# FFT and two expert layers on one core: a tensor constant in the weight conversion, sums of expert 2 kept in PSUM

## Chip, core and metric

The kernel runs on one core of one Trainium2 chip, as a single program. The metric is the device time of one execution in microseconds (us). TensorE (PE) multiplies matrices, with its weight loads (PEld) beside them; VectorE (DVE), ScalarE (ACT) and GpSimd (POOL) work element by element; SyncE (SP) issues the DMAs. Each engine takes its instructions in order and waits on semaphores. Matmuls write to PSUM, eight banks of 128 partitions x 512 fp32; everything else lives in SBUF.

## The reference

```python
X = np.fft.fft(np.fft.fft(x, axis=1), axis=2).real      # x: (2, 3008, 256)
x = X.reshape(6016, 256)
h = x @ w_in                                            # expert 1: 256 -> 2048
x = (h / (1 + np.exp(-h))) @ w_out                      # silu, 2048 -> 256
h = x @ w_in2                                           # expert 2
y = (np.maximum(h, 0) + alpha * np.minimum(h, 0)) @ w_out2
```

The weights come as float64.

## The kernel before

The kernel holds everything transposed, features on partitions and tokens along the free dimension. A value that must keep fp32 accuracy is split into a high and a low part (`hi`, a rounded copy made by ScalarE; `lo`, the difference, made by VectorE or GpSimd), and a product is three matmuls: hi by hi, hi by lo, lo by hi.

**Stages.** The DFT of batch 0 takes the first 40 us. Expert 1 runs from there to about 448 us, as 96 steps of 16 feature tiles x 6 token chunks of `CW` = 502 columns; in it the DFT of batch 1 and all weight conversions are spread by a table of step numbers (`PLAN`), and a scheduler orders each engine's instructions. Expert 2 runs from 448 us to the end, in an order written out by hand.

**Conversion from float64** (`to_f32`). A weight block of 128x512 arrives as two 32-bit words for each value. Five steps make fp32 of it: `zero` (ScalarE: absolute value of the high word), `one` (VectorE: maximum with a constant), `two` (VectorE: shift left by 3 and mask), `three` and `four` (VectorE: or in bits of the low word, then the sign). There are 32 such conversions of a block: 16 of expert 1's weights (tiles `cvi`, `cvo`), between 17 and 166 us, and 16 of expert 2's (`v2w`, `v2o`), between 258 and 415 us. Expert 1's steps meanwhile need VectorE three times each: `t` (from the PSUM tile `pe`), `hp` and again `t` (from `po`); GpSimd makes `gl`, the low parts, most of the time.

**Expert 2.** There are 96 passes of the loop, each for one pair of feature tiles `n`. The first layer is a fast 2x2 block product: seven block products (`product(n, j, ...)`, three matmuls of 252 columns each) in place of eight, with block sums formed by the other engines. All of pass `n` shares one bank `ac` (two halves of 252 columns) and uses one more, `b`:

- `outer(n)`: products 1 and 5 into the halves of `ac`; ScalarE copies both halves to `e` in SBUF.
- `inner(n)`: product 2 into `b`, product 6 added to the first half of `ac`, product 3 to the second. `h11`: VectorE adds `b` and `e` to a part of `h0`. `h12`: ScalarE copies the first half of `ac` to `u`, then VectorE adds it to the second half, into the other part of `h0`.
- `seventh(n)`: product 7 onto the first half of `ac`, then copied to `u`; `h22`: VectorE adds `u` and `e` into a part of `h1`. `fourth(n)`, in the next pass: product 4 onto the first half of `ac`, which is the rest of `h1`.
- `absolute` and `prelu`: the activation as a*h + |b*h|, |b*h| (`q`) by ScalarE, the sum by VectorE; once for `h0` (502 columns) and twice for `h1` (252 columns out of SBUF, 250 straight out of `ac`).
- `high2`, `low2`: the split of the result (`gh`, `gl`); `mm4`: the second layer, 12 matmuls of 502 columns in each pass, into two banks that are written out (`ot`, `out_t`) every eight passes.

In each pass TensorE issues: products 1 and 5, six matmuls of the second layer, product 4 of the pair before, products 2, 6 and 3, six matmuls of the second layer, product 7.

Of the kernel before, what the change touches and what calls it, by code (L numbers as in the profile page):

```python
# [122 lines left out]
def fft_moe_kernel(  # L123
# [337 lines left out]
    def prep_o1(g):  # L461
        pieces = []

        def high(h, v):
# [8 lines left out]
        for h in range(2):
            v, st = to_f32(None, (f"o{g}", h * 512, 512), f"o{g}_{h}")
# [241 lines left out]
    W = CW - HALF  # L716

    def outer(n):

        h = H[n] = {}  # L720
        h["ac"] = mm_ps(f"ac{n}", 2 * HALF)
# [2 lines left out]
        h["e"] = work(F32, f"e{n}", 2 * HALF)
        nc.scalar.activation(h["e"], h["ac"], AF.Copy)

    def inner(n):

        h = H[n]
        h["b"] = mm_ps(f"b{n}", HALF)  # L730
        product(n, 2, h["b"], True)
# [2 lines left out]
        h["u"] = work(F32, f"u{n}", 2 * HALF)
        h["h0"] = work(F32, f"h0_{n}")

    def h11(n):
        h = H[n]
        nc.vector.tensor_tensor(h["h0"][:, :W], h["b"][:, :W], h["e"][:, :W], op=ALU.add)

    def h12(n):
        h = H[n]
        nc.scalar.activation(h["u"][:, :HALF], h["ac"][:, :HALF], AF.Copy)  # L743
        nc.vector.tensor_tensor(h["h0"][:, R], h["ac"][:, HALF:], h["u"][:, :HALF], op=ALU.add)

# [13 lines left out]
    PART = {0: (0, slice(0, CW)), 1: (1, R), 2: (1, slice(0, W))}  # L759

    def source(n, part):
        i, to = PART[part]
        return H[n]["ac"][:, :W] if part == 2 else H[n][f"h{i}"][:, to]

    def absolute(n, part):

        i, to = PART[part]
        h = H[n]
        if ("q", i) not in h:
            h["q", i] = work(F32, f"q{i}_{n}")  # L770
        nc.scalar.activation(h["q", i][:, to], source(n, part), AF.Abs, scale=coef(n, i, 1))  # L771

    def prelu(n, part):
        i, to = PART[part]
# [49 lines left out]
    if True:  # L824
        with tc.manual_schedule():
            zero = conv(F32, "zero")
            nc.vector.memset(zero[:, :256], 0.0)
# [132 lines left out]
        with tc.manual_schedule():  # L960
# [102 lines left out]
```

## Time and profile before

| | us |
|---|---|
| median of 3 runs | 961.2 (961.08 to 964.77) |
| the profiled execution, its own time | 962.4 |
| its span, first to last instruction | 960.5 |
| PE busy | 948.8 (99%) |
| DVE busy | 791.4 (82%) |
| ACT busy | 708.0 (74%) |
| POOL busy | 418.2 (44%) |

The chain of work that ended last is PE for 87% of the span. A matmul's recorded duration contains its latency, and the next one starts before it ends, so PE's work is read better from the distance between starts: two matmuls of 502 columns start 0.23 us apart, two of 252 columns 0.115 us. The granted clock of TensorE is 0.999 of full speed over the span.

### The profile page before, as it was taken

Reading aid. Unit: us, or ns where it says so; the run is one execution under the profiler, and the core shown is the slowest. Engines: PE = TensorE matmul, PEld = TensorE weight load, DVE = VectorE, ACT = ScalarE, POOL = GpSimd, SP = SyncE. Lnnn points to the kernel's source line nnn. Section 1 sums busy time; section 2 is a strip of 40 time slices with the busy share of each in tenths; the row PEclk is TensorE's granted clock in tenths of the full one; section 3 lists DMA queues with packets and bytes.
Section 4 is the critical chain, followed back from the end, with each engine's and each line's share of the span. In section 5 each row is a group of like instructions: output and inputs, shape, how many; then the busy total and the mean of one; then the engine's idle time right before and its main releaser. Section 6 shows DMA issues by size and latency. Waiting matters only on the chain.

```text
span 960.5 us, 14540 instructions
## 1 busy us (share of the span) xinstructions
PE 948.8 (99%) x5236; PEld 823.8 (86%) x5236; DVE 791.4 (82%) x1334; ACT 708.0 (74%) x1413; POOL 418.2 (44%) x363
## 2 busy tenths in 40 slices
PE   9999999999999999999999999999999999999998
PEld 6887887788888888888899999999999999999997
DVE  6889999987778888996978888787878878787876
ACT  3676756675566766686888788788878888887885
POOL 2376969953266776798622122122212212221200
PEclk9999999999999999999999999999999999999999
DMA  8811110207121311100200100020020001000000
GB/s 273 251 71 44 45 45 4 83 14 234 46 102 45 118 58 43 44 0 1 86 1 23 63 3 23 1 66 14 9 65 1 23 1 65 23 1 22 1 22 22
DMA packets 17767, 49.39 MB, mean 51 GB/s; under 512 B 1824, under 2 KB 11296, under 8 KB 15648
## 3 DMA queue, kind: packets, MB, share of 16 engines
q1 hardware_dynamic: 17696, 48.47, 15.0%
q8 instruction: 41, 0.67, 0.3%
q14 instruction: 30, 0.25, 0.1%
HBM read 32.98 MB, written 15.48 MB: 50 GB/s over the span
## 4 chain that ended last, share of the span: by engine, by line
PE 87%; DVE 4%; POOL 2%; ACT 2%; DMA 2%; issue 2%; SPq 1%; ACTq 0%; POOLq 0%; DVEq 0%
PE a L807 27%; PE ac L709 20%; PE a L635 8%; PE a L637 8%; PE a L639 8%; PE b L709 3%; PE po L576 2%; PE po L578 2%; PE pe L576 2%; PE pe L578 2%; PE pe L577 2%; PE po L577 2%; DMA ys<-ya 1%; POOL gl L613 1%; PE psb L330 1%
## 5 line engine op out<-in xcount | busy, mean ns | idle before, releaser
L807 PE MATMUL a<-gh,wo 128*128 128x502 f32 x768 | 268.2, 391 | 0.0
L807 PEld LDWEIGHTS a<-gh,wo 128*128 128x128 f32 x768 | 144.9, 189 | 23.0
L613 POOL TENSOR_TENSOR gl<-t,gh 128x502 fp32r<-128x502 f32 x96 | 133.2, 1388 | 58.5 <-ACT t L601 46.4
L776 DVE SCALAR_TENSOR_TENSOR h<-h,fc,q 128x502 f32<-128x502 f32 x192 | 124.9, 650 | 33.9 <-ACT q L771 30.4
L807 PE MATMUL a<-gl,wo 128*128 128x502 f32 x384 | 149.8, 391 | 0.1
L787 DVE TENSOR_TENSOR gl<-h,gh 128x502 fp32r<-128x502 f32 x192 | 146.2, 762 | 0.1
L600 ACT ACTIVATE gh<-hp 128x502 fp32r<-128x502 f32 x96 | 59.9, 624 | 105.8 <-DVE hp L594 105.5
L637 PE MATMUL a<-gl,wo 128*128 128x502 f32 x384 | 133.7, 391 | 0.1
L639 PE MATMUL a<-gh,wo 128*128 128x502 f32 x384 | 133.4, 391 | 0.0
L635 PE MATMUL a<-gh,wo 128*128 128x502 f32 x384 | 124.3, 391 | 0.6 <-DVE o L644 0.4
L782 ACT ACTIVATE gh<-h 128x502 fp32r<-128x502 f32 x192 | 118.4, 617 | 2.9 <-DVE h L776 2.8
L771 ACT ACTIVATE q<-h,fc 128x502 f32<-128x502 f32 x192 | 116.9, 609 | 2.4 <-DVE h L754 1.3
L613 POOL TENSOR_TENSOR gl<-hp,gh 128x502 fp32r<-128x502 f32 x63 | 88.9, 1411 | 57.2 <-ACT hp L601 45.9
L591 DVE SCALAR_TENSOR_TENSOR t<-n,sm,pe 128x502 f32<-128x502 f32 x96 | 70.2, 731 | 24.6 <-PE pe L578 23.6
L695 POOL TENSOR_TENSOR os<-o1r,os 128x252 fp32r<-128x252 f32 x36 | 33.1, 933 | 122.6 <-ACT os L694 122.6
L637 PEld LDWEIGHTS a<-gl,wo 128*128 128x128 f32 x384 | 72.4, 189 | 15.7 <-POOL gl L613 0.9
L635 PEld LDWEIGHTS a<-gh,wo 128*128 128x128 f32 x384 | 71.8, 189 | 15.5 <-ACT hp L601 0.8
L639 PEld LDWEIGHTS a<-gh,wo 128*128 128x128 f32 x384 | 72.4, 189 | 14.6
L685 POOL TENSOR_TENSOR xt<-o1r 128x252 f32<-128x252 f32 x24 | 17.7, 742 | 154.1 <-DVE h L776 150.5
L807 PEld LDWEIGHTS a<-gl,wo 128*128 128x128 f32 x384 | 72.5, 189 | 8.4 <-DVE gl L787 0.6
L743 ACT ACTIVATE u<-ac 128x252 f32<-128x252 f32 x96 | 36.6, 382 | 54.4 <-PE ac L709 54.4
L594 DVE TENSOR_TENSOR hp<-t,po 128x502 f32<-128x502 f32 x96 | 64.5, 672 | 12.6 <-PE po L578 8.5
(173 smaller groups left out, 2299.0 us busy)
## 6 DMA issues: line engine op xcount, KB each, us to landing
od<-o SPq DMA_DIRECT2D x6, 1004.0 KB, 4.8
o1r<-od SPq DMA_DIRECT2D x6, 1004.0 KB, 5.7
out_t<-ot SPq DMA_DIRECT2D x24, 251.0 KB, 2.6
x<-in_xs SPq DMA_DIRECT2D x8, 512.0 KB, 5.4
raw_w<-in_wi SPq DMA_DIRECT2D x4, 1024.0 KB, 7.8
raw_w<-in_wo SPq DMA_DIRECT2D x4, 1024.0 KB, 5.7
raw_i<-in_wi SPq DMA_DIRECT2D x3, 1024.0 KB, 4.8
raw_o<-in_wo SPq DMA_DIRECT2D x3, 1024.0 KB, 6.6
```

The lines of the kernel that those rows point to most:

```text
L591: nc.vector.scalar_tensor_tensor(t, E128[c], odd_sb[:, f : f + 1], pe, op0=ALU.mult, op1=ALU.add)
L594: nc.vector.tensor_tensor(hp, t, po, op=ALU.add)
L613: LAST["gl", i] = (nc.gpsimd if s or lo_pool(i + 1) else nc.vector).tensor_tensor(lo, h, hi.bitcast(F32), op=ALU.subtract)
L635: nc.tensor.matmul(ACC1[lb, s], hi, G[i, s][0], start=st, stop=False)
L637: nc.tensor.matmul(ACC1[lb, s], hi, G[i, s][1], start=False, stop=False)
L639: nc.tensor.matmul(ACC1[lb, s], lo, G[i, s][0], start=False, stop=sp)
L709: nc.tensor.matmul(to, w, x, start=start and q == 0, stop=q == 2, skip_group_check=True)
L771: nc.scalar.activation(h["q", i][:, to], source(n, part), AF.Abs, scale=coef(n, i, 1))
L776: nc.vector.scalar_tensor_tensor(h[f"h{i}"][:, to], source(n, part), coef(n, i, 0), h["q", i][:, to], op0=ALU.mult, op1=ALU.add)
L782: nc.scalar.activation(hi, H[n][f"h{i}"], AF.Copy)
L787: nc.vector.tensor_tensor(lo, H[n][f"h{i}"], G[n, i][0].bitcast(F32), op=ALU.subtract)
L807: nc.tensor.matmul(ACC2[lb], w[lb][j], x, start=st and first, stop=sp and last)
```

## The change

In the conversion, for all blocks but the first three, step `one` becomes a VectorE operation on two tensors (the second a constant `km` of one column, read again for each element), and step `two` takes its mask from the same constant tile. The two constants are written by two small memsets at the start.

In expert 2, ScalarE copies the first half of `ac` (product 1) to the bank `b` itself, and product 2 is accumulated there by TensorE, so `h11` is no longer needed; product 2 now comes last of the three inner ones. `h12` writes its sum into the second half of `b`, `h22` writes into the second half of `ac`. Both activations then read one bank of 504 columns; the two halves overlap by two columns, which the host removes. The second layer and the output have 504 columns in place of 502.

```diff
-    def to_f32(dst, raw, n):
+    def to_f32(dst, raw, n, alone=False):
...
         def one():
             t = box[0].bitcast(F32)
-            nc.vector.tensor_scalar(t, t, F64_AT_F32_ZERO, None, op0=ALU.max)
+            if alone:
+                nc.vector.tensor_scalar(t, t, F64_AT_F32_ZERO, None, op0=ALU.max)
+            else:
+                nc.vector.tensor_tensor(t, t, km[:, :1].to_broadcast([128, w]), op=ALU.max)
 
         def two():
             t = box[0]
-            nc.vector.tensor_scalar(t, t, 3, 0x3FFFFFF8, op0=ALU.logical_shift_left, op1=ALU.bitwise_and)
...
+                mask = km.bitcast(U32)[:, 1:2].to_broadcast([128, w])
+                nc.vector.scalar_tensor_tensor(
+                    t, t, 3, mask, op0=ALU.logical_shift_left, op1=ALU.bitwise_and
+                )
...
-        h["e"] = work(F32, f"e{n}", 2 * HALF)
-        nc.scalar.activation(h["e"], h["ac"], AF.Copy)
+        h["e"] = work(F32, f"e{n}", HALF)
+        nc.scalar.activation(h["b"][:, :HALF], h["ac"][:, :HALF], AF.Copy)
+        nc.scalar.activation(h["e"], h["ac"][:, HALF:], AF.Copy)
...
-        h["b"] = mm_ps(f"b{n}", HALF)
-        product(n, 2, h["b"], True)
         product(n, 6, h["ac"][:, :HALF], False)
         product(n, 3, h["ac"][:, HALF:], False)
...
+        product(n, 2, h["b"][:, :HALF], False)
-    def h11(n):
-        h = H[n]
-        nc.vector.tensor_tensor(h["h0"][:, :W], h["b"][:, :W], h["e"][:, :W], op=ALU.add)
...
-        nc.vector.tensor_tensor(h["h0"][:, R], h["ac"][:, HALF:], h["u"][:, :HALF], op=ALU.add)
+        nc.vector.tensor_tensor(h["b"][:, HALF:], h["ac"][:, HALF:], h["u"][:, :HALF], op=ALU.add)
...
-        nc.vector.tensor_tensor(h["h1"][:, R], h["u"][:, HALF:], h["e"][:, HALF:], op=ALU.add)
+        nc.vector.tensor_tensor(h["ac"][:, HALF:], h["u"][:, HALF:], h["e"], op=ALU.add)
...
+        nc.scalar.activation(h["q", i], h["b" if i == 0 else "ac"], AF.Abs, scale=coef(n, i, 1))
...
-                    absolute(n - 1, 1)
                     high2(n - 1, 0)
...
-                    prelu(n - 1, 1)
                     fourth(n - 1)
-                    absolute(n - 1, 2)
+                    absolute(n - 1, 1)
                 if new:
                     inner(n)
-                    h11(n)
                 if old:
-                    prelu(n - 1, 2)
+                    prelu(n - 1, 1)
```

TensorE in the middle of a pass of expert 2 (pair 50; `ws0_4` are the weights of product 4, and so on; what a row waits for stands in brackets). Before:

```order
L709 MATMUL ac49_7674<-os6_0_7357,ws0_4h_3122 128x252 [waits Activation_49]
L709 MATMUL ac49_7674<-os6_1_7358,ws0_4h_3122 128x252
L709 MATMUL ac49_7674<-os6_0_7357,ws0_4l_3123 128x252
L709 MATMUL b50_7774<-os6_0_7357,ws0_2h_3655 128x252 [waits PE_49]
L709 MATMUL b50_7774<-os6_1_7358,ws0_2h_3655 128x252
L709 MATMUL b50_7774<-os6_0_7357,ws0_2l_3656 128x252
L709 MATMUL ac50_7743<-os6_0_7357,ws0_6h_4190 128x252 [waits Activation_49]
L709 MATMUL ac50_7743<-os6_1_7358,ws0_6h_4190 128x252
L709 MATMUL ac50_7743<-os6_0_7357,ws0_6l_4191 128x252
```

The same place after the change:

```order
L720 MATMUL ac49_7580<-os6_0_7273,ws0_4h_3125 128x252 [waits DVE_49]
L720 MATMUL ac49_7580<-os6_1_7274,ws0_4h_3125 128x252
L720 MATMUL ac49_7580<-os6_0_7273,ws0_4l_3126 128x252
L720 MATMUL ac50_7647<-os6_0_7273,ws0_6h_4193 128x252 [waits Activation_49]
L720 MATMUL ac50_7647<-os6_1_7274,ws0_6h_4193 128x252
L720 MATMUL ac50_7647<-os6_0_7273,ws0_6l_4194 128x252
L720 MATMUL ac50_7647<-os6_0_7273,ws0_3h_4275 128x252
L720 MATMUL ac50_7647<-os6_1_7274,ws0_3h_4275 128x252
L720 MATMUL ac50_7647<-os6_0_7273,ws0_3l_4276 128x252
L720 MATMUL b50_7648<-os6_0_7273,ws0_2h_3658 128x252 [waits PE_49]
```

Product 2 moved behind products 6 and 3, and product 4 waits for VectorE (`h22`, which now writes the same bank) where it waited for ScalarE.

VectorE in the same passes, from the `h12` of one pair to that of the next. Before:

```order
L744 TENSOR_TENSOR h0_49_7714<-ac49_7674,u49_7713 128x252 [waits Activation_49]
L787 TENSOR_TENSOR gl2_48_0_7723<-h0_48_7653,gh2_48_0_7690 128x502
L776 SCALAR_TENSOR_TENSOR h0_49_7714<-h0_49_7714,fc_82,q0_49_7721 128x502 [waits Activation_49]
L754 TENSOR_TENSOR h1_49_7753<-u49_7713,e49_7681 128x252 [waits Activation_49]
L787 TENSOR_TENSOR gl2_48_1_7755<-h1_48_7684,gh2_48_1_7719 128x502
L776 SCALAR_TENSOR_TENSOR h1_49_7753<-h1_49_7753,fc_82,q1_49_7757 128x252 [waits Activation_49]
L739 TENSOR_TENSOR h0_50_7785<-b50_7774,e50_7750 128x250 [waits PE_49]
L776 SCALAR_TENSOR_TENSOR h1_49_7753<-ac49_7674,fc_82,q1_49_7757 128x250 [waits Activation_49]
L744 TENSOR_TENSOR h0_50_7785<-ac50_7743,u50_7784 128x252 [waits Activation_49]
```

After:

```order
L748 TENSOR_TENSOR b49_7581<-ac49_7580,u49_7620 128x252 [waits PE_49,Activation_49]
L782 TENSOR_TENSOR gl2_48_0_7627<-h0_48_7591,gh2_48_0_7596 128x504
L771 SCALAR_TENSOR_TENSOR h0_49_7658<-b49_7581,fc_82,q0_49_7625 128x504 [waits Activation_49]
L757 TENSOR_TENSOR ac49_7580<-u49_7620,e49_7588 128x252 [waits Activation_49]
L782 TENSOR_TENSOR gl2_48_1_7661<-h1_48_7618,gh2_48_1_7623 128x504
L771 SCALAR_TENSOR_TENSOR h1_49_7687<-ac49_7580,fc_82,q1_49_7676 128x504 [waits Activation_49]
L748 TENSOR_TENSOR b50_7648<-ac50_7647,u50_7689 128x252 [waits PE_49,Activation_49]
```

Nine instructions became seven: the add of `b` and `e` is gone, and one activation sum of 504 columns, right in front of `h12`, stands for two of about half the size.

VectorE in expert 1, where the second block of the second group of first-layer weights (`cvi_1`) begins. Before:

```order
L187 TENSOR_SCALAR cvi_0_538<-cvi_0_538 128x512 [waits Activation_49]
L595 TENSOR_TENSOR t_523<-t_523,po_504 128x502 [waits DVE_49]
L187 TENSOR_SCALAR cvi_1_542<-cvi_1_542 128x512 [waits Activation_49]
L191 TENSOR_SCALAR cvi_0_538<-cvi_0_538 128x512 [waits DVE_49]
L350 TENSOR_TENSOR z_2_439<-psb_0_12_544,z_2_439 128x376 [waits Activation_49]
```

After:

```order
L191 TENSOR_TENSOR cvi_0_541<-cvi_0_541,km 128x512 [waits Activation_49]
L606 TENSOR_TENSOR t_526<-t_526,po_507 128x502 [waits DVE_49]
L191 TENSOR_TENSOR cvi_1_545<-cvi_1_545,km 128x512 [waits Activation_49]
L199 SCALAR_TENSOR_TENSOR cvi_0_541<-cvi_0_541,km 128x512 [waits DVE_49]
L361 TENSOR_TENSOR z_2_442<-psb_0_12_547,z_2_442 128x376 [waits Activation_49]
```

The order is the same here and the operations are of another kind; elsewhere in expert 1 the scheduler moves single instructions of VectorE and TensorE by a few places.

## Rows read from the trace of the kernel before

**Rows 1.** The profile's page, part 1: busy us, share of span, instructions.

```profile
PE 948.8 (99%) x5236; PEld 823.8 (86%) x5236; DVE 791.4 (82%) x1334; ACT 708.0 (74%) x1413; POOL 418.2 (44%) x363
```

**Rows 2.** Waits over the whole span: us in total, times, longest.

```profile
PEld ac L709 <- DVE h L744: 2.1, 3, 0.9
...
PE po L576 <- DVE t L595: 1.8, 1, 1.8
```

**Rows 3.** Busy us of each engine by stretch, then clock and DMA.

```profile
50.00:170.00 120.00, 117.24 (x552) 97.70 (x551) 111.17 (x150) 80.83 (x149) 96.00 (x77) 1.00 0.12 41
...
110.00:130.00 20.00, 20.00 (x102) 17.03 (x101) 19.10 (x28) 14.65 (x28) 16.97 (x14) 1.00 0.11 45
...
150.00:170.00 20.00, 19.08 (x93) 15.92 (x94) 19.08 (x23) 12.89 (x25) 19.53 (x15) 1.00 0.09 27
...
448.00:480.00 32.00, 31.01 (x186) 26.84 (x185) 25.27 (x48) 24.19 (x55) 18.76 (x19) 1.00 0.18 65
480.00:955.00 475.00, 475.00 (x3019) 430.64 (x3018) 381.23 (x734) 385.82 (x807) 97.49 (x95) 1.00 0.06 22
```

**Rows 4.** Timeline of one pass of expert 2: start, duration, engine, line, operation.

```profile
749.91 0.40 PE L709 MATMUL ac<-os,ws_4h 128*128 128x252 f32 x2
...
750.47 0.47 ACT L771 ACTIVATE q<-ac,fc 128x250 f32<-128x250 f32 x1 [0.22 <-PE ac L709]
...
751.15 0.47 DVE L776 SCALAR_TENSOR_TENSOR h<-ac,fc,q 128x250 f32<-128x250 f32 x1
...
751.98 0.42 DVE L744 TENSOR_TENSOR h<-ac,u 128x252 f32<-128x252 f32 x1 [0.37 <-ACT u L743]
...
752.44 0.72 ACT L771 ACTIVATE q<-h,fc 128x502 f32<-128x502 f32 x1
...
752.67 0.39 PE L709 MATMUL ac<-os,ws_7h 128*128 128x252 f32 x2
...
753.06 1.05 ACT L164 ACTIVATE ot<-a 128x502 f32<-128x502 f32 x2
...
754.00 0.38 ACT L749 ACTIVATE u<-ac 128x252 f32<-128x252 f32 x1
...
754.41 0.47 DVE L754 TENSOR_TENSOR h<-u,e 128x252 f32<-128x252 f32 x1 [0.40 <-ACT u L749]
...
755.09 0.40 PE L709 MATMUL ac<-os,ws_4h 128*128 128x252 f32 x2
```

**Rows 5.** Timeline: the one late product 7 after 480 us.

```profile
705.58 0.42 DVE L744 TENSOR_TENSOR h<-ac,u 128x252 f32<-128x252 f32 x1 [0.64 <-ACT u L743]
...
706.06 0.50 PE L709 MATMUL ac<-os,ws_7h 128*128 128x252 f32 x2
```

**Rows 6.** Groups by line and shape: busy us, mean ns of one.

```profile
L591 DVE SCALAR_TENSOR_TENSOR t<-n,sm,pe 128x502 f32<-128x502 f32 x96 | 70.2, 731 | 24.6 <-PE pe L578 23.6 <-ACT n L361 0.6
...
L725 ACT ACTIVATE e<-ac 128x504 f32<-128x504 f32 x96 | 56.7, 591 | 17.3 <-PE ac L709 16.5
...
L776 DVE SCALAR_TENSOR_TENSOR h<-ac,fc,q 128x250 f32<-128x250 f32 x96 | 44.8, 467 | 0.4 <-ACT q L771 0.4
...
L743 ACT ACTIVATE u<-ac 128x252 f32<-128x252 f32 x96 | 36.6, 382 | 54.4 <-PE ac L709 54.4
```

**Rows 7.** Timeline at the start of expert 2: `h22` and product 4.

```profile
467.95 0.95 DVE L754 TENSOR_TENSOR h<-u,e 128x252 f32<-128x252 f32 x1
...
468.21 0.40 PE L709 MATMUL ac<-os,ws_4h 128*128 128x252 f32 x2
```

**Rows 8.** Conversion steps by line: duration ns min/median/max, first and last start.

```profile
L187 DVE TENSOR_SCALAR cvo<-cvo x8: 412/856/5059, 25.1 to 152.1; 128x512 f32<-128x512 f32 x8
...
L195 DVE SCALAR_TENSOR_TENSOR cvo<-raw_o,cvo x8: 679/1106/1671, 26.0 to 160.4; 128x512 uint32<-128x512 uint32 x8
```

**Rows 9.** Timeline in expert 1: GpSimd behind a two-tensor step and behind `one`.

```profile
96.64 1.73 POOL L613 TENSOR_TENSOR gl<-t,gh 128x502 fp32r<-128x502 f32 x1
...
99.69 1.47 POOL L613 TENSOR_TENSOR gl<-hp,gh 128x502 fp32r<-128x502 f32 x1
```

More of the change, by code (lines that the diff above doesn't have):

```diff
@@ L64 @@
 PAIRS = [(k0 + i, k0 + (k1 - k0) // 2 + i) for k0, k1 in zip(K_PARTS, K_PARTS[1:]) for i in range((k1 - k0) // 2)]
+EXP_MANT = float(np.uint32(0x3FFFFFF8).view(np.float32))
 F64_AT_F32_ZERO = float(np.uint32(0x38000000).view(np.float32))
@@ L149, in work @@
     def work(dt, name, w=CW):
-        return kp.tile([128, w], dt, tag="wk", name=name, padded_shape=[128, 504])
+        return kp.tile([128, w], dt, tag="wk", name=name, padded_shape=[128, 2 * HALF])
     def conv(dt, name):
@@ L186, in one @@
             t = box[0].bitcast(F32)
-            nc.vector.tensor_scalar(t, t, F64_AT_F32_ZERO, None, op0=ALU.max)
+            if alone:
+                nc.vector.tensor_scalar(t, t, F64_AT_F32_ZERO, None, op0=ALU.max)
+            else:
+                nc.vector.tensor_tensor(t, t, km[:, :1].to_broadcast([128, w]), op=ALU.max)
         def two():
             t = box[0]
-            nc.vector.tensor_scalar(t, t, 3, 0x3FFFFFF8, op0=ALU.logical_shift_left, op1=ALU.bitwise_and)
+            if alone:
+                nc.vector.tensor_scalar(t, t, 3, 0x3FFFFFF8, op0=ALU.logical_shift_left, op1=ALU.bitwise_and)
+            else:
+                mask = km.bitcast(U32)[:, 1:2].to_broadcast([128, w])
+                nc.vector.scalar_tensor_tensor(
+                    t, t, 3, mask, op0=ALU.logical_shift_left, op1=ALU.bitwise_and
+                )
         def three():
@@ L222, in fft_moe_kernel @@
     fc = wp.tile([128, 3, NF], F32, name="fc")
+    km = wp.tile([128, 2], F32, name="km")
     cs = wp.tile([128, CD0], F32, tag="cs", name="cs")
@@ L451, in prep_w1 @@
         for h in range(2):
-            v, st = to_f32(None, (f"i{g}", 512 * h, 512), f"i{g}_{h}")
+            v, st = to_f32(None, (f"i{g}", 512 * h, 512), f"i{g}_{h}", g == 0)
             pieces.append((st, steps(h, v)))
@@ L473, in prep_o1 @@
         for h in range(2):
-            v, st = to_f32(None, (f"o{g}", h * 512, 512), f"o{g}_{h}")
+            v, st = to_f32(None, (f"o{g}", h * 512, 512), f"o{g}_{h}", g == 0 and h == 0)
             pieces.append(
@@ L714, in coef @@
         return fc[:, j, f : f + 1]
[L716 removed]
     def outer(n):
         h = H[n] = {}
[L721 removed]
+        h["ac"], h["b"] = mm_ps(f"ac{n}", 2 * HALF), mm_ps(f"b{n}", 2 * HALF)
         product(n, 1, h["ac"][:, :HALF], True)
         product(n, 5, h["ac"][:, HALF:], False)
[L724 to L725 removed]
+        h["e"] = work(F32, f"e{n}", HALF)
+        nc.scalar.activation(h["b"][:, :HALF], h["ac"][:, :HALF], AF.Copy)
+        nc.scalar.activation(h["e"], h["ac"][:, HALF:], AF.Copy)
     def inner(n):
         h = H[n]
[L730 to L731 removed]
         product(n, 6, h["ac"][:, :HALF], False)
         product(n, 3, h["ac"][:, HALF:], False)
[L734 to L739 removed]
+        product(n, 2, h["b"][:, :HALF], False)
     def h12(n):
         h = H[n]
+        h["u"] = work(F32, f"u{n}", 2 * HALF)
         nc.scalar.activation(h["u"][:, :HALF], h["ac"][:, :HALF], AF.Copy)
[L744 removed]
+        nc.vector.tensor_tensor(h["b"][:, HALF:], h["ac"][:, HALF:], h["u"][:, :HALF], op=ALU.add)
     def seventh(n):
@@ L752, in h22, with absolute, prelu @@
         h = H[n]
-        h["h1"] = work(F32, f"h1_{n}")
-        nc.vector.tensor_tensor(h["h1"][:, R], h["u"][:, HALF:], h["e"][:, HALF:], op=ALU.add)
+        nc.vector.tensor_tensor(h["ac"][:, HALF:], h["u"][:, HALF:], h["e"], op=ALU.add)
     def fourth(n):
         product(n, 4, H[n]["ac"][:, :HALF], False)
[L759 to L767, printed above, removed]
-        h = H[n]
[L769 to L774, printed above, removed]
+    def absolute(n, i):
+        h = H[n]
+        h["q", i] = work(F32, f"q{i}_{n}", 2 * HALF)
+        nc.scalar.activation(h["q", i], h["b" if i == 0 else "ac"], AF.Abs, scale=coef(n, i, 1))
+    def prelu(n, i):
         h = H[n]
+        h[i] = work(F32, f"h{i}_{n}", 2 * HALF)
         nc.vector.scalar_tensor_tensor(
-            h[f"h{i}"][:, to], source(n, part), coef(n, i, 0), h["q", i][:, to], op0=ALU.mult, op1=ALU.add
+            h[i], h["b" if i == 0 else "ac"], coef(n, i, 0), h["q", i], op0=ALU.mult, op1=ALU.add
         )
     def high2(n, i):
-        hi = work(F32R, f"gh2_{n}_{i}")
-        nc.scalar.activation(hi, H[n][f"h{i}"], AF.Copy)
+        hi = work(F32R, f"gh2_{n}_{i}", 2 * HALF)
+        nc.scalar.activation(hi, H[n][i], AF.Copy)
         G[n, i] = [hi]
     def low2(n, i):
-        lo = work(F32R, f"gl2_{n}_{i}")
-        nc.vector.tensor_tensor(lo, H[n][f"h{i}"], G[n, i][0].bitcast(F32), op=ALU.subtract)
+        lo = work(F32R, f"gl2_{n}_{i}", 2 * HALF)
+        nc.vector.tensor_tensor(lo, H[n][i], G[n, i][0].bitcast(F32), op=ALU.subtract)
         G[n, i].append(lo)
@@ L795, in mm4 @@
             for lb in range(2):
-                ACC2[lb] = acc_ps(f"a2_{t}_{lb}")
+                ACC2[lb] = acc_ps(f"a2_{t}_{lb}", 2 * HALF)
         st, sp = p == 0 and i == 0, p == 7 and i == 1
@@ L808, in mm4 @@
             if sp and last:
-                o = work(F32, f"ot{t}_{lb}")
+                o = work(F32, f"ot{t}_{lb}", 2 * HALF)
                 evac(o, ACC2[lb], lb and t == 2 * NC - 1)
@@ L829, in fft_moe_kernel @@
             nc.vector.memset(sm, 0.0)
+            nc.vector.memset(km[:, :1], F64_AT_F32_ZERO)
+            nc.vector.memset(km[:, 1:], EXP_MANT)
             nc.scalar.activation(sm[:1, :1], sm[:1, :1], AF.Silu)
@@ L1051 @@
     ]
-    args.append(nc.dram_tensor("out_t", (2 * NC, 2, 128, CW), F32, kind="ExternalOutput").ap())
+    args.append(nc.dram_tensor("out_t", (2 * NC, 2, 128, 2 * HALF), F32, kind="ExternalOutput").ap())
     with tile.TileContext(nc, schedule_with_timeline_sim=True) as tc:
@@ L1055 @@
     r = _run(nc, [{f"in_{n}": arrays[n] for n in _IN}], core_ids=[0])
-    got = r.results[0]["out_t"].reshape(B, NCB, 2, D, CW).transpose(0, 2, 1, 4, 3)
+    got = r.results[0]["out_t"].reshape(B, NCB, 2, D, 2 * HALF)
+    got = np.delete(got, np.s_[HALF : 2 * HALF - (CW - HALF)], 4).transpose(0, 2, 1, 4, 3)
     got = got.reshape(B, 2, NCB * CW, D)[:, :, :NPAIR]
```

2 lines of the change are left out of this document (1 added, 1 removed).

## The prediction

> **What bounds the kernel now.** I read the page first, then the waits, then busy time by stretch. TensorE is busy for 948.8 of 960.5 us [rows 1]. That figure alone proves little, because a matmul's record holds its latency, but the other two views say the same: from 480 us to 955 us TensorE is busy for every microsecond of the 475, and from 50 to 170 us for 117.24 of 120 [rows 3]. In the list of waits, what TensorE lost to others is a handful of entries: 1.8 us once in expert 1, where product `po` waited for VectorE's `t`, and three waits of product 7 on `h12` in expert 2, 2.1 us together [rows 2]. So VectorE and ScalarE are not the bound, and work taken from them can win at most the few microseconds that TensorE waits: 120 - 117.24 = 2.8 in the tight part of expert 1, and 1.0 (by busy time) to 2.1 (by waits) at the start of expert 2. The question is rather what the new order makes TensorE wait for, 96 times.
>
> **Columns.** The second layer gets 504 columns for 502. Per pass 12 matmuls, 96 passes: 1,152 matmuls. Product 4 starts at 749.91 and product 7, behind 9 matmuls of 252 columns and 6 of 502 (and product 4's own 3), at 752.67 [rows 4]: 2.76 us for 12 x 252 + 6 x 502 = 6,036 columns, 0.457 ns a column. Two columns are 0.91 ns, times 1,152 is **+1.0 us**. Nothing hides it, since TensorE has no gap there.
>
> **Product 7 behind `h12`.** This is the tightest chain of a pass. Before: product 4 starts at 749.91, ScalarE's `q` of 250 columns begins 0.56 later at 750.47 and ends at 750.94, VectorE's sum starts 0.21 after that and takes 0.47, `h12` ends at 752.40, and product 7 starts at 752.67, without a gap [rows 4]. After the change `q` and the sum are 504 wide and both stand in front of `h12`. From rows: `q` takes 0.468 at 250 columns; ScalarE's copies out of PSUM of 252 and 504 columns differ by 591 - 382 = 209 ns, 0.83 ns a column [rows 6], so 254 more columns make 0.47 + 0.21 = 0.68. VectorE's sum out of PSUM takes 467 ns at 250 columns and, as another sum of the same kind with an operand in PSUM, 731 at 502 [rows 6]: 0.73 at 504. A following add starts some 0.08 before the recorded end of the one ahead and takes 0.42. So `h12` ends at 749.91 + 0.56 + 0.68 + 0.21 + 0.73 - 0.08 + 0.42 = 752.43, against 752.40 now. The removed add `h11` stood ahead of that sum and cost nothing on this chain. The copy to `u` comes earlier, since product 2 moved behind products 6 and 3.
>
> How late may it end? In the one late case `h12` ended at 706.00; product 7 is recorded from 706.06, and its first two matmuls take 0.50 in place of 0.39 [rows 5, 4]. So TensorE really goes on 0.06 + 0.11 = 0.17 after the add. Due at 752.67, product 7 is late if `h12` ends after 752.50. The slack is **0.07 us**, so I cost this at nothing; but it is small, and it is used 95 times.
>
> What I cannot price is `h12` writing to PSUM: no VectorE or ScalarE instruction of the trace writes there. Below: 0.42 as now (a gain is excluded, since the product's due time doesn't move). Above: the nearest row is the add of the same size between two SBUF tiles, 0.47 [rows 4], so +0.05, still inside the slack; the farthest is 0.95 [rows 7], where GpSimd was in the way. I take 0.42, because that add's slow cases read two SBUF tiles and `h12` reads one.
>
> [...]
>
> **Product 4 behind `h22`.** Product 4 now waits for VectorE's add into the other half of its bank; it waited for ScalarE's copy `u`. It is short in the pass behind an output (11 of them): two copies of the output stand on ScalarE ahead of `u`: `q` 0.72, `ot` 1.05, `u` 0.38, then `h22` at 754.41, ending 754.88, with product 4 due at 755.09 [rows 4]. After: the split of the sum before `h12`, which stands ahead of that `q` on ScalarE, can start only 0.06 after the sum's end (752.09 by the chain above), so at 752.15; it takes 0.62, and `q` starts 0.10 before it ends, at 752.67, in place of 752.44. With `q` at 0.68, `u` starts 0.19 to 0.20 later (754.20), and `h22` ends at 755.08. By the same 0.17, it had to end by 754.92: 0.16 late, 11 times, **+1.8 us**. Behind product 4 queue products 6, 3 and 2 and all of the pass. Ends: 0 (if `h22` is not slowed by GpSimd: 0.42 and an earlier `u`), 3.2 (if the add's write to PSUM costs 0.13 more).
>
> **Start of expert 2.** The waits of product 7 there (2.1 us) come from VectorE being held up. They go away, because the sum is now one and reads PSUM. But `h22` at 467.95 took 0.95 and ended at 468.90, while product 4 started at 468.21 [rows 7]; now product 4 would be 0.69 + 0.17 = 0.86 late, in two passes. One replaces the other: **0**, ends -2.1 and +1.0.
>
> **Conversions.** Free of other engines, the old steps `one` and `two` take 0.41 and the two-tensor steps 0.68 [rows 8]. That is +0.27 us for each of 2 x 29 operations on VectorE. The longest is 5.06 against 1.67: one step stood that long behind four GpSimd operations, and from it comes the 1.8 us wait of `po` [rows 8, 2]. No two-tensor step waited so long, so I take **-1.8 us**.
>
> Against it: 24 of the new operations fall between 50 and 170 us, 24 x 0.27 = 6.5 us, less 3.4 from the long case, on a VectorE that is busy for 111.2 of 120 [rows 3]. On the average that fits. By stretches it does not: from 110 to 130 us it is busy 19.10 of 20 and gets four of them, 1.1 more, from 150 to 170 us 19.08 and gets as much [rows 3]. In the first of these TensorE lost nothing, in the second 0.9. I take **+2.0 us**, ends 0 and 6.5. The 32 operations after 258 us lie on a VectorE with a tenth of its time free, and cost nothing; without that cover they'd be 8.6. GpSimd's next operation takes 1.73 behind a two-tensor step and 1.47 behind `one` [rows 9]; from 150 to 170 us GpSimd is busy for 19.53 of 20 [rows 3] and four such steps fall there: 4 x 0.26 = 1.0 at most, and I take **+0.5**.
>
> The two memsets lie in the wait for the first input.
>
> **Sum.** 1.0 + 1.8 + 0 + 0 - 1.8 + 2.0 + 0.5 = +3.5 us. The profiled execution took 962.4 us, so it would take 965.9; it lies 1.2 above the median of the runs, 961.2, so I predict **964.7 us** for the median. A measurement of this kernel tells about 0.5%, 4.8 us, from no change: faster is below 956.4, slower above 966.0.
>
> **Rivals.**
>
> A. `h12` ends late in every pass. It decides from 0.07 us on. At 0.17 (its write to PSUM that much dearer, or ScalarE late with `q`) 95 passes lose 0.1 each, +9.5: 974.2 us. For it: the slack is a tenth of a `q`. Against: prices from rows fit inside. 14%.
>
> B. Expert 1 becomes VectorE's: all 6.5 us of the new operations reach TensorE, and GpSimd's 1.0. Sum 1.0 + 1.8 - 1.8 + 6.5 + 1.0 = +8.5: 969.7 us. For it: 95% busy stretches. Against: from 110 to 130 us TensorE lost nothing at 95%. 18%.
>
> C. On the other side: the waits end and no new ones come, because VectorE has one operation in nine less to hold it up in each pass and nothing starves behind GpSimd. -1.8, -2.1 at the start of expert 2, -0.9 from 150 to 170 us, +1.0 for columns: -3.8, 957.4 us. It decides if `h22` ends before 754.92 in the output passes and the scheduler finds room in expert 1. 20%.
>
> D. The constant tensor does not take the starvation away, and the rest hides: +1.0 and +1.8, 964.0 us. 8%.
>
> My own case has 40%, between 962.5 and 967.5.
>
> **Numbers.** Case C's end and half of A lie outside 957.5 to 972; that leaves out about 2 in 10. Faster by over 0.5%: only if C goes beyond its sum, 6%. Slower by over 0.5%: A and B, 32%, and the upper part of my own case, 6%: 38%. Within 0.5%: 56%.
>
> **What would show it.** The group of the second layer's matmuls with 504 columns and the same mean within 2 ns; product 7 starting 2.76 us after product 4, and `h12` ending 2.5 us after it; product 4 waiting for `h22` about 0.16 us in 11 passes and in two at the start; no conversion step over 2 us; VectorE at 97% or more from 110 to 170 us, with waits of TensorE there of 1 to 3 us. I am wrong if product 7 waits for VectorE in most passes (A), if TensorE loses more than 5 us between 50 and 190 us (B), or if both stretches are free of waits (C).

## The result, and the profile after

The changed kernel took **969.5 us** (median of 4 runs, 968.56 to 970.34). Beside it the kernel before took 962.5 (4 runs, 961.08 to 964.77; the 961.2 from which I forecast was the median of three of them). The ratio is 1.0071, with a 95% interval of 1.0045 to 1.0096. So the change costs 4.3 to 9.2 us, where I had forecast 3.5 and had thought no measurable loss likelier than a loss.

The page of the profiled execution, part 1 (busy us, share of span, instructions; its span is 967.9 us, and the execution took 969.72), against [rows 1]:

```profile
PE 954.1 (99%) x5236; PEld 822.8 (85%) x5236; DVE 744.9 (77%) x1144; ACT 696.5 (72%) x1413; POOL 423.0 (44%) x363
```

VectorE has 46 us of work and 190 instructions less, because expert 2 needs less of it, and the kernel is slower all the same. The loss lies ahead of expert 2. In the timelines of the two kernels, its first product starts 7.7 us later, while expert 2's length, from there to the last matmul, is 507.9 against 507.7 us. Before:

```profile
448.15 0.39 PE L709 MATMUL ac<-os,ws_1h 128*128 128x252 f32 x2
```

After:

```profile
455.88 0.40 PE L720 MATMUL ac<-os,ws_1h 128*128 128x252 f32 x2
```

To see where in expert 1, I took the time from each matmul's start to the next one's, less the steady step of its size (0.116 us for 252 columns, 0.228 for 502, 0.233 for 512; other sizes are left out), and added up the rest by stretches of 20 us. From 60 to 80 us TensorE now loses 0.2 where it lost 2.3. From 140 to 180 us it loses 7.8 (1.25 before), and from 400 to 440 us 3.1 (0.0 before). These make -2.0 + 6.6 + 3.1 = 7.7; what the other stretches gain and lose nearly cancels. The list of waits names what it waits for (against [rows 2]; total, times, longest; the main rows of expert 1):

```profile
PEld a L646 <- ACT gh L611: 5.7, 7, 2.3
...
PEld po L587 <- DVE t L606: 4.5, 6, 1.0
...
PEld a L648 <- POOL gl L624: 2.8, 6, 1.0
...
PE a L646 <- DVE t L606: 1.8, 1, 1.8
PE po L587 <- DVE t L606: 1.8, 5, 0.5
```

These rows are expert 1's chain: the second layer `a` waits for `gh`, which ScalarE makes from VectorE's `hp` and `t`, or for GpSimd's `gl`; and a new product `po` waits until VectorE's `t` has read the one before. Of [rows 2], product 7's wait for `h12` is gone. Busy time by stretch, against [rows 3]:

```profile
130.00:150.00 20.00, 17.92 (x75) 13.30 (x73) 18.85 (x24) 11.53 (x21) 13.67 (x11) 1.00 0.16 53
150.00:170.00 20.00, 18.48 (x84) 15.05 (x85) 18.05 (x21) 12.21 (x24) 20.00 (x15) 0.91 0.00 1
400.00:448.00 48.00, 46.62 (x199) 36.70 (x198) 44.15 (x58) 38.21 (x76) 41.07 (x35) 1.00 0.06 22
480.00:955.00 475.00, 474.79 (x3024) 430.02 (x3023) 321.99 (x554) 376.77 (x815) 98.43 (x101) 1.00 0.06 22
```

In the last, expert 2, TensorE has no gap worth the name and VectorE 59 us less than before. In the first three VectorE isn't at 100% anywhere; GpSimd is, from 150 to 170 us. What happens between 140 and 151 us shows in the timeline of VectorE and, at its end, of TensorE:

```profile
140.72 3.43 DVE L199 SCALAR_TENSOR_TENSOR cvi<-cvi,km 128x512 uint32<-128x512 uint32 x2
144.07 0.67 DVE L605 TENSOR_TENSOR hp<-t,po 128x502 f32<-128x502 f32 x1
...
145.86 0.66 DVE L606 TENSOR_TENSOR t<-t,po 128x502 f32<-128x502 f32 x1
146.45 2.15 DVE L209 SCALAR_TENSOR_TENSOR cvi<-raw_i,cvi 128x512 uint32<-128x512 uint32 x2
148.52 0.73 DVE L602 SCALAR_TENSOR_TENSOR t<-n,sm,pe 128x502 f32<-128x502 f32 x1
...
150.76 0.71 PE L646 MATMUL a<-gh,wo 128*128 128x502 f32 x2 [1.83 <-DVE t L606]
```

Two steps `two` in a row take 3.43 us, where undisturbed they take 0.68 each (before, the same two took 1.83, from 138.85); `hp` and `t`, for which ScalarE and then TensorE wait, stand behind them. Over the stretch from 40 to 448 us, the groups of steps `one` and `two` (busy us, mean ns) are now:

```profile
L199 DVE SCALAR_TENSOR_TENSOR v2o<-v2o,km 128x512 uint32<-128x512 uint32 x8 | 10.3, 1292 | 0.1
L199 DVE SCALAR_TENSOR_TENSOR cvo<-cvo,km 128x512 uint32<-128x512 uint32 x7 | 9.9, 1410 | 0.0
L191 DVE TENSOR_TENSOR v2o<-v2o,km 128x512 f32<-128x512 f32 x8 | 8.9, 1112 | 2.8 <-ACT v2o L184 2.8
L199 DVE SCALAR_TENSOR_TENSOR v2w<-v2w,km 128x512 uint32<-128x512 uint32 x8 | 8.8, 1098 | 0.0
L199 DVE SCALAR_TENSOR_TENSOR cvi<-cvi,km 128x512 uint32<-128x512 uint32 x6 | 8.1, 1361 | 0.0
L191 DVE TENSOR_TENSOR v2w<-v2w,km 128x512 f32<-128x512 f32 x8 | 7.1, 883 | 1.3 <-ACT v2w L184 1.2
L191 DVE TENSOR_TENSOR cvo<-cvo,km 128x512 f32<-128x512 f32 x6 | 6.9, 1156 | 4.4 <-ACT cvo L184 4.4
L191 DVE TENSOR_TENSOR cvi<-cvi,km 128x512 f32<-128x512 f32 x6 | 6.1, 1019 | 2.7 <-ACT cvi L184 2.7
```

They add up to 66.1 us for 57 steps; the eight groups before add up to 48.3. No mean is near 0.68: on average a step loses about half a microsecond. The old steps lost nearly as much: 48.3 / 57 = 0.85 us each, where undisturbed they take 0.41.

Expert 2's chain, in the timeline of the pass that answers to [rows 4] (the one behind an output):

```profile
757.66 0.40 PE L720 MATMUL ac<-os,ws_4h 128*128 128x252 f32 x2
...
758.21 0.68 ACT L766 ACTIVATE q<-ac,fc 128x504 f32<-128x504 f32 x1 [0.55 <-PE ac L720]
...
758.93 0.74 DVE L771 SCALAR_TENSOR_TENSOR h<-ac,fc,q 128x504 f32<-128x504 f32 x1 [1.51 <-ACT q L766]
...
759.59 0.42 DVE L748 TENSOR_TENSOR b<-ac,u 128x252 f32<-128x252 f32 x1
...
760.40 0.39 PE L720 MATMUL ac<-os,ws_7h 128*128 128x252 f32 x2
...
762.16 0.43 DVE L757 TENSOR_TENSOR ac<-u,e 128x252 f32<-128x252 f32 x1 [0.49 <-ACT u L753]
...
762.84 0.40 PE L720 MATMUL ac<-os,ws_4h 128*128 128x252 f32 x2
```

`h12` (759.59) ends 2.35 us after product 4's start and product 7 follows at 2.74 without a gap; `h22` (762.16) ends 0.25 ahead of the next product 4. Nothing is late.

### The profile page after: what moved, and what is told of

It is laid out like the page before. It is cut to its first block, busy times and chain, and to the rows that moved or that the text cites. A ratio compares the mean times of both kernels' runs of the same rounds, so it can differ in the third digit from the quotient of the medians.

```text
span 967.9 us, 14405 instructions
## 1 busy us (share of the span) xinstructions
PE 954.1 (99%) x5236; PEld 822.8 (85%) x5236; DVE 744.9 (77%) x1144; ACT 696.5 (72%) x1413; POOL 423.0 (44%) x363
## 4 chain that ended last, share of the span: by engine, by line
PE 87%; DVE 7%; issue 2%; ACT 2%; POOL 1%; DMA 0%; SPq 0%; DVEq 0%; ACTq 0%; POOLq 0%
PE a L802 27%; PE ac L720 21%; PE a L648 7%; PE a L650 7%; PE a L646 7%; PE b L720 3%; PE pe L587 2%; PE pe L589 2%; PE pe L588 2%; PE po L589 2%; PE po L587 2%; PE po L588 2%; PE psb L341 1%; PE psa L297 1%; DVE t L602 1%
## 5 line engine op out<-in xcount | busy, mean ns | idle before, releaser
L802 PE MATMUL a<-gh,wo 128*128 128x504 f32 x768 | 268.0, 391 | 0.0
L771 DVE SCALAR_TENSOR_TENSOR h<-ac,fc,q 128x504 f32<-128x504 f32 x96 | 71.3, 743 | 123.2 <-ACT q L766 123.2
L624 POOL TENSOR_TENSOR gl<-t,gh 128x502 fp32r<-128x502 f32 x96 | 138.0, 1438 | 59.7 <-ACT t L612 41.9
L802 PE MATMUL a<-gl,wo 128*128 128x504 f32 x384 | 149.7, 391 | 0.0
L777 ACT ACTIVATE gh<-h 128x504 fp32r<-128x504 f32 x192 | 120.4, 627 | 40.2 <-DVE h L771 40.2
L782 DVE TENSOR_TENSOR gl<-h,gh 128x504 fp32r<-128x504 f32 x192 | 145.4, 758 | 0.1
L648 PE MATMUL a<-gl,wo 128*128 128x502 f32 x384 | 137.5, 394 | 0.8 <-POOL gl L624 0.6
L650 PE MATMUL a<-gh,wo 128*128 128x502 f32 x384 | 135.7, 392 | 0.0
L646 PE MATMUL a<-gh,wo 128*128 128x502 f32 x384 | 124.9, 394 | 3.2 <-DVE t L606 1.8
L771 DVE SCALAR_TENSOR_TENSOR h<-b,fc,q 128x504 f32<-128x504 f32 x96 | 71.3, 743 | 29.0 <-ACT q L766 28.9
L766 ACT ACTIVATE q<-ac,fc 128x504 f32<-128x504 f32 x96 | 65.5, 682 | 38.9 <-PE ac L720 38.1
L605 DVE TENSOR_TENSOR hp<-t,po 128x502 f32<-128x502 f32 x96 | 64.5, 672 | 7.6 <-PE po L589 2.7
```

The lines of the kernel that those rows point to most:

```text
L605: nc.vector.tensor_tensor(hp, t, po, op=ALU.add)
L624: LAST["gl", i] = (nc.gpsimd if s or lo_pool(i + 1) else nc.vector).tensor_tensor(lo, h, hi.bitcast(F32), op=ALU.subtract)
L646: nc.tensor.matmul(ACC1[lb, s], hi, G[i, s][0], start=st, stop=False)
L648: nc.tensor.matmul(ACC1[lb, s], hi, G[i, s][1], start=False, stop=False)
L650: nc.tensor.matmul(ACC1[lb, s], lo, G[i, s][0], start=False, stop=sp)
L766: nc.scalar.activation(h["q", i], h["b" if i == 0 else "ac"], AF.Abs, scale=coef(n, i, 1))
```

## Experiments

**Theory 1**: the new conversion operations themselves cost the time, through VectorE and GpSimd in expert 1. **Rivals**: expert 2's new waits are the loss (2); the scheduler's new order in expert 1 is the loss (3). A ratio is that of a run to the kernel before on the same chip; 0.1% is 0.96 us.

### The two halves of the change apart

The first kernel is the one before with the new conversion; the second is the changed one with the old conversion everywhere:

```diff
-    def to_f32(dst, raw, n, alone=False):
+    def to_f32(dst, raw, n, alone=True):
```

The other two are the changed kernel with the new conversion for one group of blocks alone (`True` as last argument for the other group).

> The new conversion in the kernel before, expert 2 as it was. The order of every engine's instructions in expert 1 is the same as in the changed kernel, so this is its expert 1 in front of the old expert 2. Theory 1 (the conversions cost the whole 7 us): 7 to 8 us above the kernel before, about 969.5, with the first product of expert 2 at 455 to 456 us. Rival (the new waits of expert 2, product 4 behind the sum written to its bank, are the loss): within 1.5 us of the kernel before.

> The changed expert 2 behind the old conversion; every engine's order in expert 1 is that of the kernel before. Theory 1: within 1 us of the kernel before (the trace of the changed kernel gives expert 2 a length of 507.9 us against 507.7), first product of expert 2 at 448.1 us. Rival (expert 2's waits are the loss): 6 to 8 us slower. Third possibility, a gain: the late product 7 at the start of expert 2 goes away, 1 to 2 us faster.

> The changed kernel with the new conversion steps only in the blocks of expert 1's weights (before 170 us); expert 2's weights are converted by the old steps. Theory 1, by stretches of the trace: +4.3 from 140 to 160 us and +2.3 from 160 to 180, -2.0 from 60 to 80, so 4 to 5 us above the kernel before, about 967. Rival (whatever the scheduler does with the new order decides, and the parts don't add up): any sum of the two halves that differs by over 2 us from the whole.

> The changed kernel with the new conversion steps only in the blocks of expert 2's weights (258 to 415 us). Theory 1, by stretches of the trace: 1.7 from 400 to 420 us, 1.4 from 420 to 440, 0.7 from 440 to 460, less 1.4 given back from 460 to 480: 2 to 4 us above the kernel before, about 965. By the prediction's own step these 32 operations cost nothing: within 1 us.

| kernel | median us | ratio (95%) |
|---|---|---|
| new conversion, old expert 2 | 973.5 | 1.0122 (1.0104 to 1.0141) |
| old conversion, new expert 2 | 959.9 | 0.9991 (0.9980 to 1.0001) |
| new conversion for expert 1's weights, new expert 2 | 965.9 | 1.0052 (1.0036 to 1.0067) |
| new conversion for expert 2's weights, new expert 2 | 964.3 | 1.0027 (1.0017 to 1.0037) |

The conversion is the whole loss, and both groups of blocks have a share: against the second kernel 5.9 and 3.5 us, together 9.4, where the whole change lies 7.7 above it (the difference is inside the 2 us that I had allowed). Expert 2's change alone measures 0.9 us faster, with an interval that just reaches no change. The first run missed its number: 11.7 us in place of 7 to 8. Its first product of expert 2 comes at 456.80, a little later than expected, and its expert 2 takes 509.8 us in place of 507.7. A small part of that is product 7, whose waits for `h12` were 2.1 us before [rows 2]:

```profile
PEld ac L720 <- DVE h L755: 2.7, 5, 0.9
```

The rest is not traced. In the second kernel these waits are gone, and product 4 waits for `h22` at the start of expert 2 in their place:

```profile
PEld ac L720 <- DVE ac L757: 1.4, 4, 0.6
```

### The operations or their order

The scheduler orders expert 1 by its own estimate of each operation, so the new steps also moved others: of expert 1's instructions, some 45 of VectorE's 500 and 330 of TensorE's 1,840 stand elsewhere when the two traces are laid side by side. Here each of the four computing engines is held to a given order in expert 1 by edges that ask for an order of issue and no wait (`PIN` is the list of instructions):

```diff
+        for order in PIN:
+            row = [seen[f"I-{n}"] for n in order if f"I-{n}" in seen]
+            for a, b in zip(row, row[1:]):
+                tc.add_manual_dep(b, a.name, mybir.DependencyInfo(mybir.DependencyClass.NoSync, mybir.DependencyReason.DATA), reason="pin")
```

> The changed kernel, new conversion steps and all, but every engine held in expert 1 to the order of instructions that the kernel before has (order edges without a wait). Theory 1 (the new operations themselves, longer and in GpSimd's way): 5 to 9 us above the kernel before, as the changed kernel (+6.8). Theory 3 (the scheduler's new order, in which TensorE's second-layer matmuls and VectorE's sums stand elsewhere): within 1.5 us of the kernel before or below it.

> The changed expert 2 with the old conversion steps, but every engine held in expert 1 to the order of instructions that the changed kernel has. Theory 1: within 1.5 us of the kernel before, since the old steps are short wherever they stand. Theory 3: 5 to 8 us above it, as the changed kernel, with TensorE's waits again from 140 to 180 and from 400 to 460 us.

> The old order of expert 1 held, the changed expert 2, and only step one (the maximum) on two tensors. Theory 1, in proportion to VectorE's time: half of what both steps cost in the old order, 3 to 4 us above the run with the old conversion (which lies 1.1 below the kernel before), so +2 to +3. Theory 3: the same as with the old conversion, -1.

> As the run before, with only step two (shift and mask) on two tensors. Theory 1: the other half, +2 to +3 us against the kernel before. Theory 3: -1. If one of the two steps costs all of it, the place of that step and not VectorE's time decides.

| operations, order (all with the new expert 2) | median us | ratio (95%) |
|---|---|---|
| new steps, old order | 968.5 | 1.0067 (1.0054 to 1.0081) |
| old steps, new order | 960.3 | 0.9987 (0.9978 to 0.9995) |
| `one` new, old order | 961.6 | 1.0009 (0.9999 to 1.0018) |
| `two` new, old order | 961.8 | 1.0009 (1.0001 to 1.0017) |

Theory 3 falls: the order costs nothing with the old steps, and the new steps cost as much in the old order. The first product of expert 2 tells the same. New steps in the old order:

```profile
453.99 0.40 PE L721 MATMUL ac<-os,ws_1h 128*128 128x252 f32 x2
```

Old steps in the new order:

```profile
447.18 0.40 PE L721 MATMUL ac<-os,ws_1h 128*128 128x252 f32 x2
```

The dose is not straight: either step alone costs 1.7 us (1.0009 less 0.9991), both together 7.3. I had expected 3 to 4 for each. My reading is that the free time of VectorE and GpSimd took up most of the first half and that the second half found no room; no run tests it.

### VectorE's time, or GpSimd's way

Two causes are left in theory 1: the time on VectorE (1a), and that two-tensor steps and GpSimd's operations keep each other waiting (1b). Both kernels below keep the old steps and the old order and add one VectorE operation of 200 columns behind each step. In the first it reads one tensor:

```diff
+                nc.vector.tensor_reduce(km[:, at : at + 1], t[:, :200], axis=mybir.AxisListType.X, op=ALU.max)
```

In the second it reads two, and writes the values back as they are:

```diff
+                    nc.vector.tensor_tensor(t, t, km[:, :1].to_broadcast([128, 200]), op=ALU.max)
...
+                    nc.vector.scalar_tensor_tensor(
+                        t, t, 0, mask, op0=ALU.logical_shift_left, op1=ALU.bitwise_and
+                    )
```

> The changed expert 2, the old conversion steps and the old order of expert 1 held, and behind each of the 58 steps one and two an added VectorE maximum over 200 columns of the block, whose result (one column) nothing uses. It takes the place of the longer steps: about 0.27 us of VectorE each, as the new steps have over the old ones, but with one tensor read and one column written. The old step stays as short as it was in GpSimd's way. Theory 1a (VectorE's time alone): 5 to 8 us above the kernel before, as the new steps in the old order (+6.4). Theory 1b (the two-tensor steps wait for GpSimd's operations and hold them up, and that is the larger part): less than 3 us above the kernel before. In between, both count.

> As the run with the added maximum over 200 columns, at the same 58 places and in the same order, but the added operation now reads two tensors (200 columns of the block and the constant) and writes 200 columns back, which changes no value. VectorE's time grows by about as much. Theory 1b (what counts is that two-tensor operations wait for GpSimd's and hold them up): well above the added maximum (+1.3), by 3 us or more, so +4 to +8 against the kernel before. Theory 1a (VectorE's time alone): as the added maximum, +0 to +3.

> The added maximum over 200 columns once more, beside the run with two tensors on one chip, and for a trace of an execution nearer to its median (the first trace was of its slowest, 968.7). Both theories: +0.5 to +3 against the kernel before.

| added operation | median us | ratio (95%) |
|---|---|---|
| maximum, one tensor | 963.1 | 1.0013 (1.0001 to 1.0025) |
| the same, once more | 963.1 | 1.0016 (1.0002 to 1.0031) |
| two tensors | 991.5 | 1.0305 (1.0281 to 1.0330) |

The added operations by group (from 40 to 480 us), one tensor:

```profile
L191 DVE TENSOR_REDUCE km<-v2o 128x1 f32<-128x200 f32 x16 | 5.8, 362 | 0.6
L191 DVE TENSOR_REDUCE km<-v2w 128x1 f32<-128x200 f32 x16 | 5.8, 361 | 0.6
...
L191 DVE TENSOR_REDUCE km<-cvo 128x1 f32<-128x200 f32 x13 | 4.7, 362 | 0.4
...
L191 DVE TENSOR_REDUCE km<-cvi 128x1 f32<-128x200 f32 x12 | 4.3, 361 | 0.4
```

Two tensors:

```profile
L195 DVE SCALAR_TENSOR_TENSOR v2o<-v2o,km 128x200 uint32<-128x200 uint32 x8 | 7.7, 964 | 0.3
...
L192 DVE TENSOR_TENSOR cvo<-cvo,km 128x200 f32<-128x200 f32 x6 | 7.0, 1162 | 0.2
...
L192 DVE TENSOR_TENSOR cvi<-cvi,km 128x200 f32<-128x200 f32 x6 | 6.0, 1006 | 0.2
L192 DVE TENSOR_TENSOR v2w<-v2w,km 128x200 f32<-128x200 f32 x8 | 5.8, 726 | 0.3
...
L195 DVE SCALAR_TENSOR_TENSOR cvo<-cvo,km 128x200 uint32<-128x200 uint32 x7 | 5.5, 790 | 0.2
...
L192 DVE TENSOR_TENSOR v2o<-v2o,km 128x200 f32<-128x200 f32 x8 | 4.9, 617 | 0.3
L195 DVE SCALAR_TENSOR_TENSOR v2w<-v2w,km 128x200 uint32<-128x200 uint32 x8 | 4.8, 606 | 0.3
...
L195 DVE SCALAR_TENSOR_TENSOR cvi<-cvi,km 128x200 uint32<-128x200 uint32 x6 | 3.6, 596 | 0.2
```

With one tensor every group has the same mean, 361 to 362 ns: these operations did not get longer beside GpSimd, which was busy for 289 of the 408 us (the second line of the windows below). With two tensors the means run from 596 to 1162 for the same 200 columns, and the sum is 45.3 us against 20.6. Theory 1b holds, far beyond its numbers: 29 us against 1.2 to 1.5.

Two things stand beside that. The second operation also writes 200 columns where the first writes one, and no run tells that from the second input. And part of the 29 us is TensorE's granted clock, which stood at half in four stretches of that trace (from 80, 172, 421 and 445 us, 20.5 us in all). Busy time, with the clock behind the five engines, with two tensors and then with one:

```profile
40.00:448.00 408.00, 387.57 (x1719) 315.36 (x1719) 360.24 (x522) 249.47 (x455) 259.15 (x207) 0.98 0.19 64
...
40.00:448.00 408.00, 403.63 (x1847) 334.40 (x1846) 364.27 (x555) 275.61 (x509) 289.43 (x234) 1.00 0.19 64
```

Half the clock for 20.5 us costs at most some 10 us, by estimate from these windows; the 19 that are left are still far above 1.2 to 1.5.

The added maximum also sizes the change itself. It puts 20.6 us on VectorE and costs 2 to 2.4 us (1.0013 and 1.0016 less 0.9991). The new steps in the old order put 18.3 us more on VectorE than the old ones (64.5 for 46.2 in the two traces) and cost 7.3. So VectorE's time by itself makes about a third (each of these numbers has an interval of one to one and a half us to either side). The rest goes with steps that, unlike the added maximum, take longer beside GpSimd, as GpSimd's operations do beside them. That as such was not new: in these two traces the old steps took 0.81 us on average for 0.41 undisturbed, the new ones 1.13 for 0.68. One part of the rest is on GpSimd's side: its `gl` of 502 columns took 1,404 ns on average with the old steps and 1,450 with the new ones (all those of GpSimd from 40 to 448 us, 156 and 153; 34 and 53 of them were over 1.6 us). In the run with the two-tensor operation added it was not longer, 1,389 ns (147 of them), so there the loss seems to come by way of VectorE. How the rest splits in the change itself, between GpSimd's delay and the uneven length of VectorE's steps, is not settled.

For the old steps, which also read one tensor, the trace of before shows it step by step: the 22 steps `one` and `two` that no GpSimd operation overlapped took 410 to 428 ns, the other 42 took 414 to 5,059, 1,017 on average. Why the added maximum stayed at 361 to 362 beside GpSimd and these did not, no run shows.

## Why the prediction was right or wrong

The time lies inside my range, at the price of rival B (969.7), not of my own case (964.7). That B came so close is partly luck: of its terms, +1.0 and +1.8 measured 0, the -1.8 was counted twice, and it put nothing after 258 us, where 3.1 were lost. By its steps:

- **Columns, +1.0: measured 0.** The second layer's matmuls at 504 columns, by group:

```profile
L802 PE MATMUL a<-gh,wo 128*128 128x504 f32 x768 | 268.0, 391 | 0.0
L802 PE MATMUL a<-gl,wo 128*128 128x504 f32 x384 | 149.7, 391 | 0.0
```

  Before, the same two groups at 502 columns were busy for 268.2 and 149.8 us, and from start to start the step is 0.228 us at both sizes. I had divided the time of a mix of 252- and 502-column matmuls by its columns, and charged two columns at that rate.
- **Product 7, 0: right, for a partly wrong reason.** `h12` takes 0.42 into PSUM as it did into SBUF, `q` 0.68 and the sum 0.74, as worked out. But I wrote "The removed add `h11` … cost nothing on this chain", and took the 0.21 us between `q` and the sum as fixed. In the trace of before, `h11` filled it:

```profile
750.81 0.42 DVE L739 TENSOR_TENSOR h<-b,e 128x250 f32<-128x250 f32 x1 [0.56 <-PE b L709]
```

  It ended at 751.23, and the sum began at 751.15 [rows 4]. Now the sum starts 0.04 behind `q`; `h12` ends 2.35 after product 4, where I had 2.52, and the slack is 0.24 in place of 0.07.
- **Product 4 behind outputs, +1.8: measured 0.** The same 0.17 us carries through: `h22` ends 0.21 to 0.28 ahead of product 4 in all 11 passes. No run shows the 0.13 that I put on the add's write to PSUM for the upper end, 3.2: `h22` took 427 ns on average into PSUM, and 433 into SBUF before.
- **Start of expert 2, 0: right in kind.** The waits of product 7 went, those of product 4 came. By the steps of TensorE's matmuls in the run with the old conversion, 1.6 us went and 0.7 came. Expert 2 as a whole: I had +2.8, and measured -0.9 (-1.9 to +0.1).
- **Starvation, -1.8: a double count.** I took the 5.06 us step as part of every execution. But it belongs to some: with the same operations in the same order, the run with the old conversion and new expert 2 shows at that place

```profile
70.53 1.40 DVE L189 TENSOR_SCALAR cvo<-cvo 128x512 f32<-128x512 f32 x1
```

  The profiled execution of before lay 1.2 above its median, and this stall is a reason near at hand: two other traces have it, 5.08 us each (new conversion for expert 2's weights alone, and the first run with the added maximum), and their executions lay 2.8 and 5.6 above their medians. Four traces with the old step and no such stall are of executions at or just below theirs. I took off the 1.2 as well as the 1.8.
- **Conversions, +2.0, +0.5 and "cost nothing" after 258 us: this step failed.** From 140 to 180 us 6.6 were lost; from 400 to 440, where I had counted on "a VectorE with a tenth of its time free", 3.1. I had the step's price from undisturbed rows (+0.27 us; 18.3 / 57 = 0.32 measured), and that was nearly right. What I had wrong is the cover. I let busy shares decide what reaches TensorE, and VectorE was busy for only 94% of either stretch. But beside GpSimd a new step takes anything from 0.7 to 1.8 us by chance (an old one 0.4 to 1.6, and 5.06 once), two in a row took 3.43, and `hp` and `t` stand behind them; GpSimd's `gl` took longer beside the new steps as well, 1,450 ns for 1,404. [rows 8 and 9] held both signs of it: a median of 1106 for 679 undisturbed, and GpSimd's 1.73.

Rival A didn't occur, nor did D. C was nearly right about expert 2 (0.7 us of new waits came) and wrong about expert 1. B had its sign, over 5 us lost between 50 and 190 us, but not its mechanism as I put it: VectorE was busy for 90 to 94% from 110 to 170 us, not for 97%.

The version with the old conversion and the new expert 2 is the best of those run: 0.9991 (0.9980 to 1.0001), and in the other order of expert 1 0.9987 (0.9978 to 0.9995), about a microsecond below the kernel before.

## What to carry to other kernels

Before making a VectorE operation longer by a second tensor in SBUF, look at GpSimd in the same stretch: here steps of either form lost 0.4 to 0.5 us each beside it, and the spread of such rows, not the undisturbed duration, tells how late what stands behind them can be. Free time by average (a tenth of VectorE) was no cover here for operations that stand ahead of what the bound engine waits for: 3.1 us were lost from 400 to 440. And ask of a stall in a profiled execution whether every execution has it, before counting its end as a gain.

## What the hardware showed that I had not expected

**A clock that fell behind a wait, and cost nothing.** Behind TensorE's wait of 1.83 us at 150.76 the granted clock fell to 0.50 of full speed for 3.4 us, from 152.49 to 155.91. From 152.54 to 155.22 six matmuls of 502 columns took 2.68 us, where six steps of 0.228 make 1.4: over a microsecond that no list of waits shows. It fell alike in the run with the new conversion for expert 1's weights. In the run with the new conversion and the old expert 2, whose expert 1 is the same, TensorE waits the same 1.83 us at 150.74, and the clock stays at 1.00. The windows of the changed kernel, and then of that run (the clock stands behind the busy times of the five engines):

```profile
153.00:154.00 1.00, 1.00 (x4) 0.74 (x4) 0.03 (x1) 1.00 (x3) 1.00 (x2) 0.50 0.00 0
...
156.00:160.00 4.00, 4.00 (x29) 3.65 (x27) 4.00 (x5) 1.80 (x4) 4.00 (x4) 1.00 0.02 4
...
153.00:154.00 1.00, 1.00 (x7) 0.80 (x6) 0.07 (x1) 1.00 (x3) 1.00 (x2) 1.00 0.00 0
...
156.00:160.00 4.00, 2.71 (x19) 2.29 (x17) 4.00 (x5) 1.35 (x4) 4.00 (x4) 1.00 0.02 4
```

At full clock TensorE only came earlier to its next wait: it stood for 1.29 us ahead of 159.58. Both runs come out of their next wait at the same time, 169.42 and 169.39. So the time lost at half clock was taken up by the wait behind it. What decides whether such a wait takes the clock down stays open.

**PSUM as VectorE's target costs nothing here**: adds of 252 columns take 419 ns into PSUM from PSUM and SBUF and 427 into PSUM from two SBUF tiles, against 421 and 433 into SBUF before (means of 96 each).
